# Decayed attention and two gated layers: scores in 64 by 64 quarters of TensorE's array, and two ScalarE steps put ahead of others

## The chip, the cores and the metric

The kernel runs on one core of a Trainium2 chip. The metric is the device time of one execution in microseconds (us); lower is better. The time before is 583.23 us, the median of three runs (583.21 to 583.51). The engines are named as in the profile: PE (TensorE's matmuls), PEld (its weight loads), DVE (VectorE), ACT (ScalarE), POOL (GpSimd) and SP (SyncE, which issues the loads).

## The reference

Blocked linear attention with a decay per head, then two feed-forward layers. Batch 2, 8 heads, 768 tokens, head size 64, so 1536 tokens of width 512 for the layers:

```python
for b in range(nb):                       # blocks of 64 tokens
    intra = einsum('bhic,bhjc->bhij', qb, kb) * Dmask     # the scores
    intra = einsum('bhij,bhjd->bhid', intra, vb)
    inter = einsum('bhid,bhde->bhie', qb * lam_pow, kv_state)
    out[:, :, sl] = intra + inter
    kv_state = lam_block * kv_state + einsum('bhsd,bhse->bhde', kb_dec, vb)
x = act1(x @ w_in) @ w_out                 # act1: 0, x, or (x + 1)^2 / 4 between
x = (sigmoid(x @ w_gate) * (x @ w_val)) @ w_out2
```

## The kernel before

**Attention** works in chunks of 128 tokens (P), not 64. A unit is one pair of heads and three chunks (CU = 3); there are 16 units, and a loop over k = 0 to 7 takes two units in each turn. A turn issues on PE, in this order: `values` (L1041, scores times v, out tile x), `updates` (L998, state sums uu), `values`, then `scores` (L980) of the two units of the next turn, then `queries` (L1061, q times the state, added to x). The scores of turn 0's units are computed ahead of the loop, so that seven turns (k = 0 to 6) hold scores. In turns 6 and 7 matmuls of the first layer (L258 to L260) stand between them, after the scores too; from turn 0 to turn 5 queries follow scores directly. The operands are fp32, and each matmul of the program appears in the trace as two records of a weight load and a matmul: 12 score matmuls are 24 records.

The two heads of a pair lie in the two halves of the partitions (e = 0 and 1), each 64 deep. Scores take as stationary operand 64 partitions and 128 columns, as out tile 128 partitions in a bank per head (s0, s1): the two heads use the upper and the lower half of the array's rows. Queries have 64 partitions and 64 columns of weights, so the two heads use two quarters on a diagonal. Values and updates have 128 partitions and 64 columns: two halves of the array's columns. Groups of these shapes are told apart in the trace by "64*128", "64*64" and "128*64".

SP loads q, k and v of a unit (tile u, `u_load`, L868) into six buffers; its next load into a buffer is issued after the `values` that read it. DVE multiplies scores with the decay (`weigh`, L1009, out pT), scans the states (`states`, L1024, out sc, which queries wait for), and makes a rest of x (`low`, L1077, xl).

**The layers** split every fp32 number into a high and a low part and multiply three times. From group to group of two slices (n0, n1) the second layer runs `pair` generators a and b on PE (L502, through `product`), whose accumulators p0 and p2 are read by ACT or DVE between two products, and `project` (L314). `pair_act` makes what `project` needs: ACT copies the high part gh (L688, L695), ACT makes a sigmoid (L691), DVE makes the rests gl and a product. In one group only (n0 = 20) `forms_third` is worked off beside it, by `along`: each of its ten steps calls `begin` (DVE, L469 and L475: sums of token halves f and rests xt2l), then the step it is given, then `end` (ACT, L472: the high part xt2h of f). Everything is issued by hand in the order of the code; each engine runs its own instructions in that order.

In that group five steps of b go along with five steps of `pair_act`. Three waits of PE stand there: in `pair`, the product of s31 into p0 needs that ACT has copied p0 before (L528), the product of v into p0 after it needs the copy L533, and the product of s24 into p2 needs that DVE has read p2 (L534).

Of the kernel before, what the change touches and what calls it, by code (L numbers as in the profile page):

```python
# [15 lines left out]
B, H, S, D = 2, 8, 768, 64  # L16
NT, DM = B * S, H * D
FF1, FF2 = 2048, 1536
P = 128
# [26 lines left out]
def fused_kernel(ctx: ExitStack, tc: tile.TileContext, qkv, qd, cst, w1, w2, out):  # L46
    nc = tc.nc
    pe, act, dve, pool, sp = nc.tensor, nc.scalar, nc.vector, nc.gpsimd, nc.sync
# [129 lines left out]
    def w_forms_ready():  # L178
        for n in forms:
            if n not in ready:  # L180
                w_forms_split(n)
# [116 lines left out]
    def project(n, t, gs, first, last, now=True):  # L298
        gh, gl = gs
        two = n >= NF1  # L300
        o = 1024 if two else 512
        w_need(n, o)
        w = ws[index[n, o]]
        if first:
            accs.update({j: bank(f"a{n}_{t}_{j}", "a") for j in range(4)})
        for j in range(4):
            js = slice(j * P, (j + 1) * P)
            if two:
                ah, al = (g[j] if isinstance(g, list) else g[:, js] for g in (gh, gl))
                ops = [(ah, w[:, 0]), (ah, w[:, 1]), (al, w[:, 0])]  # L310
            else:
                ops = [(w[:, 0, js], gh), (w[:, 1, js], gh), (w[:, 0, js], gl)]
            for m, (a, b_) in enumerate(ops):
                pe.matmul(accs[j], lhsT=a, rhs=b_, start=(first and m == 0),  # L314
                          stop=(last and m == 2))
        if t == NTT - 1:
            used.update([index[n, o]] if two else [index[n, 0], index[n, o]])
        if last and now:
            flush(n, t)
# [21 lines left out]
    def x_split(t, js):  # L341
        tt = slice(t * TT, (t + 1) * TT)
        for j in js:
            o = part[t][:, j]
            act.activation(xh[:, j, tt], o, AF.Copy)
            dve.tensor_tensor(out=xl[:, j, tt], in0=o, in1=xh[:, j, tt].bitcast(F32),
                              op=ALU.subtract)
# [6 lines left out]
    def go_on():  # L354

        if not (later and later.pop(0)()):
            w_round()
# [45 lines left out]
    def form_split(f, i):  # L403
        hi, lo = x_targets()[i]
        act.activation(hi, f[i], AF.Copy)
        dve.tensor_tensor(out=lo, in0=f[i], in1=hi.bitcast(F32), op=ALU.subtract)
# [31 lines left out]
    def forms_second():  # L438


        x1, x2 = part[0][:, 0:HK], part[0][:, HK:]
        y1, y2 = part[1][:, 0:HK], part[1][:, HK:]
        for o, a, b_ in ((x1, y1, x1), (y1, y2, y1), (y2, y2, x1), (x2, x2, y2)):
            dve.tensor_tensor(out=o, in0=a, in1=b_, op=ALU.subtract)
        return [x1, y2, x2, y1]
# [254 lines left out]
    def single(n, t, between=()):  # L700
        between = iter(between)
        h = hidden(n, t, 0)
        for _ in between:
            pass
        v = hidden(n, t, 512)
        if t == NTT - 1:
            used.update((index[n, 0], index[n, 512]))
        r = rest(f"r{n}_{t}")
        act.activation(r, h, AF.Sigmoid)
        dve.tensor_tensor(out=r, in0=r, in1=v, op=ALU.mult)  # L710
        return r
# [4 lines left out]
    def second_layer(waiting):  # L716

        x_split(1, range(4))
        for p in waiting:
            project(*p)  # L720
        f = []
        later.extend([
            lambda: x_split(2, (0, 1)),
            lambda: x_split(2, (2, 3)) or f.extend(forms_second()),
            lambda: form_split(f, 0) or form_split(f, 2) or True,
            lambda: form_split(f, 1) or form_split(f, 3) or True,
        ])
        fresh = None
        for t in range(NTT):
            for n in range(NF1, NF1 + GF):  # L730
                r = single(n, t)
                if fresh:
                    behind.append(fresh[:2] + (parts(fresh[2], *fresh[:2]),) + fresh[3:])
                if len(behind) == 2:
                    project(*behind.pop(0))
                fresh = n, t, r, n == NF1, n == NF1 + GF - 1
                if (n, t) == (NF1 + GF - 1, NTT - 1):
                    break
                go_on()
                if (n, t) != (NF1, 0):  # L740
                    w_round()
        prog["forms"] = pool
        for n0 in range(NF1 + GF, NF1 + NF2, GF):
            n1 = n0 + 1
            a, b = pair(n0), pair(n1)
            next(a)
            if fresh:
                behind.append(fresh[:2] + (parts(fresh[2], *fresh[:2]),) + fresh[3:])
                waiting, fresh = behind, None
                next(a)  # L750
                next(a)
            thirds = n0 > NF1 + GF
            if not thirds:
                w_round()
            if n0 == NF1 + 2 * GF:
                made = forms_third()

            def along(step):
                begin, end = made.pop(0) if thirds and made else (None, None)
                if begin:  # L760
                    begin()
                x = step()
                if end:
                    end()
                return x

            for _ in range(4 if thirds else 2):
                along(lambda: next(a))
            prog["room"], prog["thirds"] = thirds, thirds
            for p in waiting:  # L770
                w_round()
                project(*p, now=False)
                prog["room"] = False
            flush(p[0], p[1], (0, 1))
            ra, ga = next(a), {}
            flush(p[0], p[1], (2, 3))
            prog["room"] = not thirds
            xa = pair_act(n0, ra, ga)
            for _ in range(5):
                along(lambda: next(b))  # L780
                next(xa)
            w_round()
            project(n0, 0, ga[0], True, False)
            along(lambda: None)
            assert not thirds or not made
            w_round()
            rb, gb = next(b), {}
            xb = pair_act(n1, rb, gb)
            if thirds:
                c = pair_third(n0)  # L790
                for _ in range(5):
                    next(c)
                    next(xb)
                w_round()
                project(n1, 0, gb[0], False, True)
                rc, gc = next(c), {}
                xc = pair_act(n0, rc, gc)
                for _ in range(3):
                    next(xc)
                w_forms_ready()  # L800
                project(n0, 1, ga[1], True, False)
                next(xc)
                w_round()
                next(xc)
                project(n1, 1, gb[1], False, True)
                waiting = []
                for i, n in enumerate((n0, n1)):
                    at = lambda x: [gc[j // 2][x][:, i * HT + j % 2 * P:i * HT + j % 2 * P + P]
                                    for j in range(4)]
                    waiting.append((n, 2, (at(0), at(1)), n == n0, n == n1))  # L810
                continue
            ha = single(n0, 2, xb)
            w_round()
            project(n1, 0, gb[0], False, True)
            ha = parts(ha, n0, 2)
            w_round()
            hb = single(n1, 2)
            w_round()
            project(n0, 1, ga[1], True, False)
            hb = parts(hb, n1, 2)  # L820
            project(n1, 1, gb[1], False, True)
            waiting = [(n0, 2, ha, True, False), (n1, 2, hb, False, True)]
        for p in waiting:
            project(*p)
# [4 lines left out]
    with ExitStack() as actx:  # L829
# [109 lines left out]
        S_ps, U_ps, pT, qs, kd, xs = {}, {}, {}, {}, {}, {}  # L939
# [31 lines left out]
        def scores(i):  # L971
            u = raw_u[i]
            S_ps[i] = []
            for e in range(2):
                s = bank(f"s{i}_{e}")
                S_ps[i].append(s)
            for c in range(CU):
                for e in range(2):
                    r = slice(e * D, (e + 1) * D)
                    pe.matmul(  # L980
                        S_ps[i][e][:, c * P:(c + 1) * P], lhsT=u[1][r, c * P:(c + 1) * P],
                        rhs=u[0][r, c * P:(c + 1) * P],
                        start=True, stop=True,
                    )

        def updates(i):
            u = raw_u[i]
# [92 lines left out]
        with tc.manual_schedule():  # L1080
# [8 lines left out]
            for k in range(nu // 2):  # L1089
                a, b = 2 * k, 2 * k + 1  # L1090
# [160 lines left out]
```

## Time and profile before

| what | before |
|---|---|
| median of three runs | 583.23 us |
| the profiled execution | 583.22 us |
| its span in the profile | 581.4 us |
| PE busy | 576.5 us (99%), 3218 matmul records |
| DVE busy | 454.7 us (78%) |
| ACT busy | 383.4 us (66%) |
| POOL busy | 52.4 us (9%) |
| granted TensorE clock, mean | 0.999 |
| attention | the first 58 us |

The span runs from the first to the last instruction that the profile shows; the execution's time is 1.8 us longer. "Busy" is a share over the whole span, and a matmul's record reaches to its modelled end, so records overlap: what a stage costs is read from the starts of the next stage, or from the chain of work that ended last, which cuts the overlap off.

### The profile page before, as it was taken

Reading aid. Unit: us, or ns where it says so; the run is one execution under the profiler, and the core shown is the slowest. Engines: PE = TensorE matmul, PEld = TensorE weight load, DVE = VectorE, ACT = ScalarE, POOL = GpSimd, SP = SyncE. Lnnn points to the kernel's source line nnn. Section 1 sums busy time; section 2 is a strip of 40 time slices with the busy share of each in tenths; the row PEclk is TensorE's granted clock in tenths of the full one; section 3 lists DMA queues with packets and bytes.
Section 4 is the critical chain, followed back from the end, with each engine's and each line's share of the span. In section 5 each row is a group of like instructions: output and inputs, shape, how many; then the busy total and the mean of one; then the engine's idle time right before and its main releaser. Section 6 shows DMA issues by size and latency. Waiting matters only on the chain.

```text
span 581.4 us, 8399 instructions
## 1 busy us (share of the span) xinstructions
PE 576.5 (99%) x3218; PEld 486.1 (84%) x3218; DVE 454.7 (78%) x772; ACT 383.4 (66%) x675; POOL 52.4 (9%) x60
## 2 busy tenths in 40 slices
PE   9999999999999999999999999999999999999997
PEld 8987888888888888888888888888888898898895
DVE  5988798788897978796898996688876676767555
ACT  4678785996777677777874977756655656655330
POOL 3440000000000000000000002422001112022000
PEclk9999999999999999999999999999999999999999
DMA  8983240022112222221312232222102221220014
GB/s 336 400 324 116 103 144 2 37 104 73 42 72 73 73 73 72 66 79 37 99 48 72 73 108 73 72 74 70 35 5 68 78 73 37 76 70 1 0 61 157
DMA packets 15880, 52.02 MB, mean 89 GB/s; under 512 B 1760, under 2 KB 1888, under 8 KB 15840
## 3 DMA queue, kind: packets, MB, share of 16 engines
q1 hardware_dynamic: 15696, 51.39, 25.1%
q8 instruction: 25, 0.41, 0.3%
q10 hardware_dynamic: 144, 0.10, 0.1%
q14 instruction: 15, 0.12, 0.1%
HBM read 48.33 MB, written 3.15 MB: 89 GB/s over the span
## 4 chain that ended last, share of the span: by engine, by line
PE 99%; DVE 0%; issue 0%
PE a L314 39%; PE p L502 26%; PE t L502 7%; PE h L258 6%; PE h L260 6%; PE h L259 6%; PE s L980 2%; PE x L1041 2%; PE x L1061 2%; PE uu L998 1%; PE z L889 1%; DVE part L336 0%; PE lam L897 0%; DVE zero L928 0%
## 5 line engine op out<-in xcount | busy, mean ns | idle before, releaser
L314 PE MATMUL a<-gh,w 128*128 128x512 f32 x384 | 118.4, 390 | 0.0
L314 PE MATMUL a<-w,gh 128*128 128x512 f32 x288 | 88.8, 390 | 0.0
L314 PEld LDWEIGHTS a<-gh,w 128*128 128x128 f32 x384 | 71.9, 188 | 15.3 <-ACT part L332 0.3
L336 DVE TENSOR_TENSOR part<-part,a 128x512 f32<-128x512 f32 x132 | 82.5, 681 | 2.7 <-PE a L314 2.7
L314 PE MATMUL a<-gl,w 128*128 128x512 f32 x192 | 74.7, 389 | 0.0
L258 PE MATMUL h<-xh,w 128*128 128x512 f32 x160 | 62.7, 392 | 0.0
L314 PEld LDWEIGHTS a<-w,gh 128*128 128x128 f32 x288 | 53.5, 188 | 10.7
L259 PE MATMUL h<-xh,w 128*128 128x512 f32 x160 | 62.3, 389 | 0.0
L260 PE MATMUL h<-xl,w 128*128 128x512 f32 x160 | 62.2, 389 | 0.0
L314 PE MATMUL a<-w,gl 128*128 128x512 f32 x144 | 56.0, 389 | 0.0
L124 ACT ACTIVATE wc<-raw 128x512 uint16<-128x512 uint32 x61 | 47.9, 785 | 10.5 <-DVE wr L135 10.5
L141 ACT ACTIVATE w<-wr 128x512 fp32r<-128x512 f32 x68 | 42.2, 621 | 16.8 <-DVE wr L135 16.6
L163 POOL TENSOR_TENSOR wr<-wr 128x256 f32<-128x256 f32 x16 | 13.3, 833 | 434.7 <-DVE w L145 434.1
L135 DVE CUSTOM_DVE_ANT_0 wr<-wr,wc 128x1024 uint16<-128x1024 uint16 x68 | 47.1, 692 | 5.8 <-ACT wc L125 3.2
L125 ACT ACTIVATE wc<-raw 128x512 f16<-128x512 f32 x61 | 46.9, 769 | 0.0
L145 DVE TENSOR_TENSOR w<-wr,w 128x512 fp32r<-128x512 f32 x65 | 45.2, 696 | 2.0 <-ACT w L141 1.7
L117 ACT ACTIVATE wr<-raw 128x512 f32<-128x512 f32 x68 | 45.0, 662 | 1.5 <-POOL s L172 0.9
L314 PEld LDWEIGHTS a<-gl,w 128*128 128x128 f32 x192 | 36.0, 188 | 7.5
L502 PE MATMUL p<-xh,s 128*128 128x512 f32 x128 | 39.5, 390 | 0.0
L502 PE MATMUL p<-xh,w 128*128 128x512 f32 x128 | 39.4, 389 | 0.0
L502 PE MATMUL p<-xth,s 128*128 128x512 f32 x128 | 39.4, 389 | 0.0
L258 PEld LDWEIGHTS h<-xh,w 128*128 128x128 f32 x160 | 30.0, 188 | 6.6 <-issue 0.2
(157 smaller groups left out, 1140.0 us busy)
## 6 DMA issues: line engine op xcount, KB each, us to landing
raw<-in_w SPq DMA_DIRECT2D x68, 512.0 KB, 3.4
u<-in_qkv SPq DMA_DIRECT2D x24, 384.0 KB, 8.2
out<-part SPq DMA_DIRECT2D x12, 256.0 KB, 2.1
u<-in_qkv SPq DMA_DIRECT2D x3, 768.0 KB, 8.6
part<-in_qkv SPq DMA_DIRECT2D x2, 384.0 KB, 8.4
cs<-in_cst ACTq DMA_DIRECT2D x1, 98.0 KB, 3.7
```

Of the source, the lines that this page charges most:

```text
L117: act.activation(r, hi.bitcast(F32), AF.Copy, scale=2.0 ** -112)
L124: act.activation(limb(U16)[:, :, 0], lo, AF.Copy, scale=2.0 ** -29)
L125: act.activation(limb(F16)[:, :, 1], hi.bitcast(F32), AF.Copy, scale=2.0 ** -60)
L135: eng.tensor_tensor(out=ri, in0=ri, in1=c, op=ALU.add)
L141: act.activation(ws[i][:, 0], tmps[i][0], AF.Copy)
L145: eng.tensor_tensor(out=ws[i][:, 1], in0=r, in1=ws[i][:, 0].bitcast(F32), op=ALU.subtract)
L258: pe.matmul(h, lhsT=wh, rhs=xh[:, k, tt], start=(k == 0), stop=False)
L259: pe.matmul(h, lhsT=wl, rhs=xh[:, k, tt], start=False, stop=False)
L260: pe.matmul(h, lhsT=wh, rhs=xl[:, k, tt], start=False, stop=(k == NP - 1))
L314: pe.matmul(accs[j], lhsT=a, rhs=b_, start=(first and m == 0), stop=(last and m == 2))
L336: dve.tensor_tensor(out=o, in0=o, in1=accs[j], op=ALU.add)
L502: pe.matmul(o, lhsT=a, rhs=b_, start=(start and k == 0 and m == 0), stop=(k == HK - 1 and m == 2), skip_group_check=True)
```

## The change

In `scores` each matmul is cut into two halves of its 64 weight columns (`half_`): the out tile's upper and lower 64 partitions. Per chunk there are four matmuls of 64 partitions by 64 columns, in the order (half 0, head 0), (half 0, head 1), (half 1, head 0), (half 1, head 1), each in a quarter of the array of its own; each still streams 128 columns of q. In the group where `forms_third` runs, `along` now gets b's step and `pair_act`'s step together, so `pair_act`'s instructions are issued before `end` instead of after it.

```diff
             xa = pair_act(n0, ra, ga)
             for _ in range(5):
-                along(lambda: next(b))
-                next(xa)
+                along(lambda: (next(b), next(xa)))
             w_round()
@@ in scores(i)
             for c in range(CU):
-                for e in range(2):
-                    r = slice(e * D, (e + 1) * D)
-                    pe.matmul(
-                        S_ps[i][e][:, c * P:(c + 1) * P], lhsT=u[1][r, c * P:(c + 1) * P],
-                        rhs=u[0][r, c * P:(c + 1) * P],
-                        start=True, stop=True,
-                    )
+                for half_ in range(2):
+                    for e in range(2):
+                        r = slice(e * D, (e + 1) * D)
+                        o = slice(half_ * D, (half_ + 1) * D)
+                        pe.matmul(
+                            S_ps[i][e][o, c * P:(c + 1) * P],
+                            lhsT=u[1][r, c * P + half_ * D:c * P + (half_ + 1) * D],
+                            rhs=u[0][r, c * P:(c + 1) * P],
+                            start=True, stop=True,
+                        )
```

On PE in one turn before, the end of the scores of its second unit, and what follows (s_0 and s_1 are the two heads' banks, "128x128" the out tile and "64x128" one of 64 partitions):

```order
L980 MATMUL s_0_465<-u_132 128x128
L980 MATMUL s_1_466<-u_132 128x128
L1061 MATMUL x_434<-qs_382,sc_97 64x128 x4
L1061 MATMUL x_485<-qs_395,sc_97 64x128 x6
L1041 MATMUL x_485<-pT_400,u_126 64x128 x6
```

The same place in a turn of the changed kernel (its lines stand one or two further):

```order
L981 MATMUL s_0_341<-part_79 64x128
L981 MATMUL s_1_342<-part_79 64x128
L981 MATMUL s_0_341<-part_79 64x128
L981 MATMUL s_1_342<-part_79 64x128
L1063 MATMUL x_306<-qs_241,sc_97 64x128 x4
L1063 MATMUL x_367<-qs_260,sc_97 64x128 x6
```

Each chunk has four score matmuls of half the size where it had two; nothing else moved on PE, where 1972 rows of the order became 2068.

On ACT in the group n0 = 20 before, from b's first step on (q is a copy of an accumulator p, gh the high part for `project`, xt2h and xh the high parts of the token forms f):

```order
L522 ACTIVATE q_0_4031<-p_0_4028 128x512
L688 ACTIVATE gh_0_4041<-q_0_3890 128x512
L472 ACTIVATE xt2h<-f_3906 128x256
L691 ACTIVATE q_1_3891<-q_1_3891 128x512
L528 ACTIVATE q_1_4032<-p_0_4028 128x512
L472 ACTIVATE xt2h<-f_3906 128x256 x2
L695 ACTIVATE gh_1_4042<-q_1_3891 128x512
L533 ACTIVATE q_2_4033<-p_0_4028 128x512
```

The same place in the changed kernel:

```order
L522 ACTIVATE q_0_4127<-p_0_4124 128x512
L688 ACTIVATE gh_0_4137<-q_0_3986 128x512
L691 ACTIVATE q_1_3987<-q_1_3987 128x512
L472 ACTIVATE xt2h<-f_4002 128x256
L528 ACTIVATE q_1_4128<-p_0_4124 128x512
L472 ACTIVATE xt2h<-f_4002 128x256
L695 ACTIVATE gh_1_4138<-q_1_3987 128x512
L472 ACTIVATE xt2h<-f_4002 128x256
L533 ACTIVATE q_2_4129<-p_0_4124 128x512
```

The sigmoid L691 and the copy L695 have each changed places with the token form's high part ahead of them. The orders of DVE, POOL and SP are the same in both kernels.

## Rows read from the trace of the kernel before

**Rows 1.** The page: busy times, and the shares of the last chain.

```profile
PE 576.5 (99%) x3218; PEld 486.1 (84%) x3218; DVE 454.7 (78%) x772; ACT 383.4 (66%) x675; POOL 52.4 (9%) x60
...
PE 99%; DVE 0%; issue 0%
```

**Rows 2.** The last chain over 0 to 60 us, in order: start, us, what.

```profile
8.90 1.58 PE s L980 x24
10.48 1.33 PE x L1061 x20
...
18.42 0.66 PE x L1041 x12
19.08 1.54 PE s L980 x24
20.61 1.33 PE x L1061 x20
21.95 0.81 PE x L1041 x12
22.75 0.58 PE uu L998 x20
...
33.82 1.54 PE s L980 x24
35.35 1.39 PE x L1061 x20
```

**Rows 3.** Line L868 over 27.5 to 28.1 us: one load of u, its landing.

```profile
L868 SPq DMA_DIRECT2D u<-in_qkv x1: 328/328/328, 27.8 to 27.8; - x1
...
DMA to landing us min/median/max: 6.0/6.0/6.0
```

**Rows 4.** Line L980 over 33.5 to 35.4 us: a wait in PE's sequencer.

```profile
L980 PEldq EVENT_SEMAPHORE  x1: 51/51/51, 33.8 to 33.8; - x1
```

**Rows 5.** A stretch: busy us of PE, PEld, DVE, ACT, POOL; clock; DMA share, GB/s.

```profile
29.00:34.00 5.00, 5.00 (x92) 4.59 (x94) 4.65 (x10) 3.02 (x8) 0.69 (x1) 1.00 1.04 410
```

**Rows 6.** DVE in order of time, around 29 to 35 us; idle before in brackets.

```profile
29.80 1.95 DVE L1009 TENSOR_TENSOR pT<-s,DT 128x384 f32<-128x384 f32 x4 [0.28 <-PE s L980]
...
34.39 0.81 DVE L1024 TENSOR_TENSOR_SCAN sc<-ld,uu 128x320 f32<-128x320 f32 x1
```

**Rows 7.** All waits of PE's weight loads from 60 to 420 us: total, times, longest.

```profile
PEld p L502 <- ACT q L533: 0.4, 1, 0.4
PEld a L314 <- ACT part L332: 0.3, 1, 0.3
PEld p L502 <- ACT q L528: 0.2, 1, 0.2
PEld p L502 <- DVE q L534: 0.2, 1, 0.2
```

**Rows 8.** ACT in order of time, 408 to 414 us; idle before in brackets.

```profile
408.58 0.42 ACT L472 ACTIVATE xt2h<-f 128x256 fp32r<-128x256 f32 x1 [1.25 <-DVE f L469]
408.90 0.62 ACT L691 ACTIVATE q<-q 128x512 f32<-128x512 f32 x1
409.43 0.58 ACT L528 ACTIVATE q<-p 128x512 f32<-128x512 f32 x1
...
412.89 0.42 ACT L472 ACTIVATE xt2h<-f 128x256 fp32r<-128x256 f32 x1 [1.44 <-DVE f L469]
413.21 0.62 ACT L695 ACTIVATE gh<-q 128x512 fp32r<-128x512 f32 x1
413.73 0.58 ACT L533 ACTIVATE q<-p 128x512 f32<-128x512 f32 x1
```

**Rows 9.** DVE in order of time, 413 to 416 us.

```profile
413.34 0.42 DVE L475 TENSOR_TENSOR xt2l<-f,xt2h 128x256 fp32r<-128x256 f32 x1 [0.48 <-ACT xt2h L472]
...
415.06 0.68 DVE L534 TENSOR_TENSOR q<-q,p 128x512 f32<-128x512 f32 x1
```

**Rows 10.** PE in the same stretch.

```profile
415.88 0.64 PE L502 MATMUL p<-xh,s 128*128 128x512 f32 x2
```

## The prediction, made before the changed kernel ran

> **What bounds the kernel now.** I read the page's busy times and last chain first: PE is busy 99% of the span and the chain is PE's for 99% of it [rows 1]. So only what PE does, or waits for, can move the end; DVE and ACT count where PE waits for them. Next I asked where PE waits. After attention, from 60 to 420 us, its weight loads wait four times, 1.1 us together [rows 7]; matmuls that are already queued cover a good part of that. The first 58 us are different: the chain there is made of short matmuls, one stage after the other [rows 2], while the DMA engines are full: share 1.04 at 410 GB/s [rows 5]. The change touches this stretch (scores) and three of the four waits (the group at 408 to 416 us).
>
> To read [rows 2]: values (x L1041) are 12 records with two column halves side by side, so six rounds of two. Behind updates, which have the same tile shape, they take 0.66 us: 0.11 us a round. Behind queries, another shape, the same 12 records take 0.81. Going over to a new shape with 64 weight columns thus costs 0.15. Scores: 24 records, two at a time, 12 rounds of 0.11 = 1.32; the row says 1.54, so their entry costs 0.22. Queries: 20 records, 10 rounds = 1.10; the row says 1.33, entry 0.23.
>
> **The change, part by part.** *Rounds.* A quarter matmul streams the same 128 columns as before. Before, two matmuls of half the array made a round, 12 rounds for two units; now 48 records go four at a time, again 12 rounds. If a round stays 0.11 nothing is won or lost here: the array was full before. Values and scores cut the array in two differently and I read the same 0.11 for both; no row shows four at once. Bounds: 0.11 as in these rows, or what PE has been seen to issue: updates pass 20 records in 0.58 us, 29 ns each, so four take 0.116, 12 rounds 1.39 [rows 2]. I take 0.11, since two of the rows nearest in shape agree on it, and keep 0.116 for the range.
>
> [...]
>
> *Entries.* Scores now have the tile shape of queries, and 64 weight columns. Their own entry should cost 0.15 instead of 0.22 (gain 0.07). The entry of the queries behind them, 0.23, should go; what can remain is a slower round of its own, 0.03 in all. Gain per turn: 0.07 + 0.20 = 0.27 (0.20 with rounds of 0.116, 0.30 at best). Queries follow scores directly six times, from 10.48 to 35.35 [rows 2]; the seventh scores stand before first-layer matmuls and gain 0.07 alone. Uncapped: 6 x 0.27 + 0.07 = 1.69 us.
>
> *The cap.* Not all of it passes. In the last such turn the second unit's q and k are loaded by an issue at 27.8 us that lands 6.0 us later, at 33.8 [rows 3], and PE's sequencer holds a wait that ends at 33.8 [rows 4]. The loads fill the DMA engines [rows 5] and land in order of issue, so an earlier PE doesn't make this one land sooner. The scores of that turn end at 35.35 [rows 2]; their second unit is the last 0.66 of it, so it begins at about 34.7 on the chain's scale, some 34.5 by starts. PE can come forward 0.6 to 0.7 there, no more. After the wait: 33.9, six rounds 0.66, a first load of 0.05 that nothing covers: queries begin at 34.6 instead of 35.35, 0.75 earlier. To reach the cap PE needs a lead of 0.6; the turns before give four times 0.27, and with rounds of 0.116 still 0.8, so the rounds' unknown is swallowed here. Of the queries' entry about half (0.1) lies behind their first matmul and comes on top; then 0.07 of the seventh scores: 0.92.
>
> Does DVE follow? Queries need the scan at 34.39, which ends at 35.2 [rows 6], nearly with the queries' start. DVE is dense from 29.80 on (busy 4.65 of 5.00 us, rows 5), and there it waited 0.28 for PE's scores; so it moves with the lead that PE has by then, 3 x 0.27 + 0.07 = 0.88, plus up to 0.27 of the first turn. Its scan then ends near 34.3, before 34.6: no bind. Should it move by its idle 0.28 only, queries start at 35.0 and 0.5 is left of 0.92: a lower end.
>
> The wait for ACT's L332, 0.3 on a weight load [rows 7], hangs on ACT's conversions, which hang on DVE: they come forward by 0.88 to 1.15 where PE comes 0.92. Worth 0 to 0.1; I take 0.04.
>
> *The two swaps on ACT.* Before, copy L533 (413.73) stands behind gh (413.21) behind xt2h (412.89), which waited 1.44 for DVE [rows 8]; gh had nothing to wait for. Now gh fills that idle time, L533 starts at 413.21 and ends at 413.79, 0.52 earlier. Likewise the sigmoid (408.90) goes into the 1.25 idle ahead of 408.58 and L528 starts at 409.0 or so instead of 409.43. So PE's waits of 0.4 for L533 and 0.2 for L528 [rows 7] should both go. What is late next: the product after p0's last one needs DVE's L534. It starts at 415.06 and ends at 415.74 [rows 9], and PE's product began at 415.88 [rows 10], its load having waited for L534 already [rows 7]. L534 stands on DVE behind xt2l at 413.34, which waited for the xt2h of 412.89, which waited for DVE's own sums [rows 8, 9]; the swap moves none of them. So PE can start that product no earlier than about 415.80, at most 0.1 before 415.88; and then with weights that are not loaded ahead, as at the entries above (0.1). Net between -0.05 and +0.14; I take 0, as both rows name the same end. What is swapped costs nothing: xt2h isn't ready before 408.58 and 412.89, and ACT is idle until then.
>
> *Sum.* 0.92 + 0.04 + 0 = 0.96. The profiled execution took 583.22 us (span 581.4 and 1.8 around it); the median is 583.23, so the sum stands against either: 583.22 - 0.96 = 582.26, rounded to **582.3 us**.
>
> **The rivals.** *Smaller gain* (0.10): the 0.23 belongs to the queries' strided weights or their waits, not to the change of shape; then 0.07 a turn is left, 7 x 0.07 = 0.5: 582.7. Against it: values behind updates have no entry, values behind queries have one, with the same operands [rows 2].
>
> *No cap* (0.10): the load at 33.8 comes forward with PE, and all 1.69 passes, 1.7 with L332: 581.5. Against it: a DMA share of 1.04 [rows 5].
>
> *The swap pays* (0.10): L534 ends earlier, for instance since DVE has the sigmoid and gh sooner and shifts; of the 0.8 waited in that group I would see about 0.3 more: 582.0. Against it: DVE's wait of 0.48 for xt2h stays [rows 9].
>
> *Scores twice as fast* (0.03): four tiles do four times the work of one, 12 rounds become six. Behind the cap that is worth 0.33 in the last turn and 0.66 for the seventh scores: 1.9 together, 581.3. Against it: the round is as long for 64 columns as for 64 partitions [rows 2]. [...]
>
> *Slower* (0.07): the four quarters don't run side by side, or PE can't issue them fast enough. The place is the 48 records of each turn. It decides at the point where they take more than 2.87 - 0.15 - 1.12 = 1.60 us, 33 ns a record: above it each turn loses. At two at a time they take 24 rounds, 2.64: about 1.05 lost in each of six turns, 1.25 in the seventh, and 12 rounds more, at least 1.32, in the first scores ahead of the loop: +9, 592 us. For it: no row shows four tiles at once. Against it: two tiles by rows, by columns and on the diagonal all overlap, and updates pass a record in 29 ns [rows 2]. [...]
>
> **How the numbers follow.** The forecast has 0.60, its own range 581.9 to 582.8 (rounds, DVE's lower end, L332). With the rivals: 0.10 + 0.10 + 0.10 + 0.03 + 0.07. The range 581.5 to 583.1 holds the forecast and the three small rivals, 0.90, and leaves out the last two. A measurement of this kernel tells about 0.2% from no change, 1.17 us, so faster means below 582.06: no cap, the swap that pays, the doubled scores and a little of the forecast's lower tail, 0.24. Slower is the last rival and a trifle: 0.08. The rest, 0.68, is within 0.2%: most of the forecast is, by 0.2 us.
>
> **What the profile after would show.** Right: scores of 48 records in about 1.47 on the chain, with queries behind them in 1.10 to 1.13; a new idle stretch or wait of PE in the last turn around 32.9 to 33.9; queries there at 34.6. L533 and L528 gone from PE's waits and L534 still there, with a longer wait. Wrong: scores of 2 us or more on the chain (slower), 0.7 (doubled), queries still at 1.33 (smaller gain), no wait at 33.8 in the last turn (no cap), or PE's product at 415.9 coming 0.3 earlier against its neighbours (the swap pays).

## The result: 0.9% slower, and PE stands still where nothing in the kernel holds it

The changed kernel took 588.48 us (median of 4 runs, 586.98 to 589.62) against 583.37 for the kernel before (4 runs, 583.21 to 583.51): a ratio of 1.0086, 95% interval 1.0057 to 1.0116. The forecast was 582.3 with a range to 583.1. The profiled execution of the changed kernel took 586.98 us, its span 585.1, which is 3.7 more than before. It was the shortest of the four; the two longest have a mean granted clock of 0.996 and 0.994 where the others have 1.000, and no trace shows what more they lost.

The page answers to [rows 1]. PE's busy time hardly moved, so the loss isn't in its work. The chain of after has 5% of DVE, 1% of DMA and 1% of "issue", where before it was PE's alone; of these, DVE's and DMA's shares are no loss of that size, since the chain, followed back, goes over to them at two short waits of PE (0.5 us for L534, shown further below, and 0.7 at 7 us). PE ran 192 matmuls more, each with a weight load, and the instruction queue q8 carried 27 packets (packets, MB, share of the 16 DMA engines' time).

```profile
span 585.1 us, 8783 instructions
PE 575.6 (98%) x3410; PEld 484.7 (83%) x3410; DVE 455.3 (78%) x772; ACT 384.0 (66%) x675; POOL 52.4 (9%) x60
q8 instruction: 27, 0.44, 0.3%
PE 92%; DVE 5%; issue 1%; DMA 1%; ACT 1%; SPq 0%; POOL 0%; DVEq 0%; ACTq 0%; POOLq 0%
```

The queue in the profile of before had

```profile
q8 instruction: 25, 0.41, 0.3%
```

The last chain over the first 62 us shows where the time went (start, us, what). It answers to [rows 2]; scores are now L981, values L1043, queries L1063.

```profile
18.76 0.81 PE s L981 x22
19.57 1.48 issue
21.05 1.03 PE s L981 x26
22.08 1.13 PE x L1063 x20
...
25.25 1.23 PE s L981 x35
26.48 1.17 issue
27.65 0.55 PE s L981 x11
28.30 1.12 PE x L1063 x19
...
31.47 1.47 PE s L981 x48
32.94 0.23 issue
33.17 1.40 PE x L1063 x20
...
38.13 0.94 PE x L1063 x12
39.08 0.84 issue
...
61.46 2.95 PE a L314 x12
```

Four pieces of "issue" make 1.48 + 1.17 + 0.23 + 0.84 = 3.72 us, as much as the span grew. Three lie in the middle of scores or of queries, after the 22nd or the 35th matmul of 48 or the 12th of 20, between two matmuls with the same operands; only the short third one lies where a stage begins. A stop costs more than its idle time: scores that take 1.47 undisturbed took 3.32 with the first (18.76 to 22.08) and 2.95 with the second (25.25 to 28.20). I estimate from such stages that the four cost some 5 us and that the quarters win over 1 us back elsewhere; that the idle time alone equals the growth is chance. In between, the forecast's small figures are there: scores 1.47, queries behind them 1.13.

In those pieces PE neither multiplies nor loads weights, while DVE and ACT go on, the granted clock is 1.00 and the DMA engines are full. The columns are the stretch, its length, busy us of PE, PEld, DVE, ACT and POOL, the clock, the DMA share and GB/s.

```profile
19.60:21.00 1.40, 0.00 (x0) 0.00 (x0) 1.40 (x5) 0.72 (x3) 0.04 (x1) 1.00 1.04 395
26.50:27.60 1.10, 0.00 (x0) 0.00 (x0) 1.10 (x3) 1.10 (x4) 0.56 (x1) 1.00 1.05 404
39.10:39.90 0.80, 0.00 (x0) 0.00 (x0) 0.80 (x3) 0.80 (x3) 0.80 (x2) 1.00 0.95 384
```

What links them is a count. If PE's records in the trace (weight loads and matmuls, with the few entries of its queue) are numbered in order of start, from 0, the first record after each stop is number 705, 961, 1217 and 1473: 256 apart, every time. The queue q8 moved 0.44 MB in 27 packets, 16 KB each, and 27 packets for 6,881 records are one for about 255. So I put the packets of q8 from the trace beside PE's passage over every 256th record:

```
            first record   PE busy   packet of q8   PE goes    stop   from the packet's
            of the block   until     start   end    on at             end to PE going on
after            449       14.09     10.97   12.08   14.09      -          -
                 705       19.57     18.63   19.65   21.05     1.48       1.40
                 961       26.48     25.00   26.03   27.64     1.16       1.61
                1217       32.94     30.54   31.62   33.06     0.12       1.44
                1473       39.08     37.61   38.56   39.92     0.84       1.36
before           449       17.56     13.76   14.84   17.56      -          -
                 705       24.13     20.21   21.33   24.13      -          -
                 961       31.17     26.62   27.72   31.17      -          -
                1217       40.45     33.71   34.73   40.45      -          -
```

Each stop ends 1.4 to 1.6 us after a packet has landed. In the kernel before, PE came to each of these records 2.7 us or more after the packet's end, so some 1.3 us or more to spare. My theory after this view (the supply theory): PE is fed its instructions in blocks of 256 records, the next block is asked for about when the last is begun (no trace shows the asking; in the changed kernel the packet starts 2.9 to 4.6 us after that), and while the loads fill the DMA engines it takes some 6.6 us until it can be used (7.0 from 14.09 to 21.05, 6.6 to 27.64, 5.4 to 33.06, 6.9 to 39.92). Halves used up 256 records in 6.6 to 7.0 us there, quarters in 5.0 to 5.8.

### The profile page after: what moved, and what is told of

Its sections match the earlier page's. It is cut to its first block, busy times and chain, and to the rows that moved or that the text cites. A ratio compares the mean times of both kernels' runs of the same rounds, so it can differ in the third digit from the quotient of the medians.

```text
span 585.1 us, 8783 instructions
## 1 busy us (share of the span) xinstructions
PE 575.6 (98%) x3410; PEld 484.7 (83%) x3410; DVE 455.3 (78%) x772; ACT 384.0 (66%) x675; POOL 52.4 (9%) x60
## 4 chain that ended last, share of the span: by engine, by line
PE 92%; DVE 5%; issue 1%; DMA 1%; ACT 1%; SPq 0%; POOL 0%; DVEq 0%; ACTq 0%; POOLq 0%
PE a L314 36%; PE p L502 23%; PE t L502 7%; PE h L258 6%; PE h L260 6%; PE h L259 6%; PE x L1043 2%; PE s L981 2%; PE x L1063 2%; DVE f L469 1%; DVE part L336 1%; PE uu L1000 1%; DMA u<-in_qkv 1%; DVE xt2l L475 0%; DVE wr L135 0%
```

## Experiments

Two theories stood at the start. Supply, as above; and its rival, that four tiles side by side make PE stall by itself, in the array or its banks. A third suspect, the two swaps on ScalarE, could be taken off at once.

### Which part of the change: scores alone, swap alone

The first kernel undoes the swap:

```
-                along(lambda: (next(b), next(xa)))
+                along(lambda: next(b))
+                next(xa)
```

> The quarters alone, the order on ScalarE as before. Supply theory: in the changed kernel PE stops for 1.2 to 1.5 us in the middle of scores and queries, and each stop begins at PE record 705, 961, 1217 or 1473, so 256 records (16 KB of instructions, the size of one packet of the instruction queue) apart; PE waits there for its own instructions. The swap has no part in that: 588.5 us (587 to 589.6), stops at the same record numbers. Rival, the swap costs it: 583 or a little less.

Measured: 587.51 us (586.72 to 588.07), ratio 1.0071, interval 1.0056 to 1.0086. PE stops at records 705 (1.70), 961 (1.15), 1217 (0.40) and 1473 (0.56). The second kernel has the swap and the old scores.

> The order on ScalarE of the changed kernel, scores in halves as before. Supply theory: the swap is worth nothing or up to 0.1 us: 583.1 to 583.4. Rival, the swap costs it: 587 to 589.

Measured: 583.30 us against 583.25, ratio 1.0001, interval 0.9991 to 1.0011. The whole loss is the quarters', and the swap is worth nothing that can be measured.

### Fewer loads, the same quarters

The loads of units 6 to 15 are left out; these units read unit 4's tiles.

```
+            if i >= NEARLY:
+                raw_u[i] = list(raw_u[4]) if 4 in raw_u else list(raw_u[i - 1])
+                return
             if i not in raw_u:
```

> The kernel before, but q, k and v of units 6 to 15 aren't loaded: these units read unit 4's again (their results are thus other numbers). The DMA engines are then full until about 17 us only, not 37. This is the base for the next kernel. Either theory: PE is the bound without the loads too, 583.0 to 583.4, first-layer products (L314) from about 57.5 us.

> The changed kernel with the same loads left out (units 6 to 15 read unit 4's data). Supply theory: instruction packets no longer wait among loads, no stop of PE at records 961 and 1473 and a small one at most at 705; the quarters then bring what was forecast without the cap by the loads: 1.3 to 1.7 us faster than the kernel with few loads and halves, about 581.7. Rival, four tiles side by side make PE stall by themselves (a conflict inside the array or its banks): the stops stay, 3 to 5 us slower than the kernel with few loads and halves, 587.

Measured: halves 583.30 us (ratio 1.0000, 0.9991 to 1.0010), so the loads don't bound the kernel before. Quarters 584.62 (583.87 to 586.58), ratio 1.0025, interval 1.0014 to 1.0035: neither 581.7 nor 587. The chain of the second says why:

```profile
18.65 0.81 PE s L984 x23
19.46 1.54 issue
21.00 0.97 PE s L984 x25
21.98 1.13 PE x L1066 x20
...
25.15 1.47 PE s L984 x48
26.62 1.12 PE x L1066 x20
```

The stop at record 705 is still there; the others are gone, and the turn from 21.98 to 26.62 takes 4.64 us. The windows of the same kernel (columns as above) put the change of the loads beside it:

```profile
14.00:19.00 5.00, 5.00 (x128) 4.65 (x128) 4.94 (x12) 2.66 (x7) 1.98 (x2) 1.00 1.04 411
25.00:30.00 5.00, 5.00 (x126) 4.63 (x126) 4.90 (x12) 3.58 (x9) 3.12 (x4) 1.00 0.02 5
```

The packet for record 705 started at 18.63, as in the changed kernel, with the engines full since record 449 at 14.03; those for 961 and later started 1.4 us or less after the block before theirs was begun, where it took 2.9 to 4.6 in the changed kernel. The loads ended later than the 17 us that I had expected (read in slices of 1.5 us, the engines were 90% busy or more up to 19.5), too late to help the first stop. So the next kernel leaves out the loads of units 4 to 15 (they read unit 3's), and the same was done to the kernel before.

> The changed kernel, and q, k and v of units 4 to 15 aren't loaded (they read unit 3's; results are other numbers). With units 6 to 15 left out, the stops at records 961, 1217 and 1473 were gone, but the one at 705 stayed at 1.5 us: its packet started at 18.6 us, when the loads had just run out. Now the loads end some 4 us earlier. Supply theory: the packet for record 705 starts by 16 us, no stop anywhere, every turn with quarters takes 4.64 us, 581.7 (581.3 to 582.3), against 583.3 for halves with few loads. Rival, the array or its banks stop at this place: 1.5 us at record 705 again, 584.6.

> The kernel before, and q, k and v of units 4 to 15 aren't loaded (they read unit 3's): the base for the changed kernel with these loads left out, which took 582.41. If PE bounds it as it bounds the kernel before, 583.3 (583.0 to 583.5), and the quarters are worth 0.9 once their instructions are in time. If the loads left out gain by themselves, 582.4, and the quarters are worth nothing.

Measured: quarters 582.41 us (582.17 to 582.67), ratio 0.9984, interval 0.9975 to 0.9993; halves 583.26, ratio 1.0001, interval 0.9991 to 1.0011. No stop at 705 or anywhere: its packet started at 16.0. Same matmuls, same quarters; with the instructions in time they gain 0.85 us. The rival, that the array stops by itself, falls here. The chain shows the short turn, 4.64 from 20.15 to 24.79, and then something else (its 0.40 of "issue" stands ahead of DVE's pT, while PE is busy):

```profile
18.68 1.47 PE s L985 x48
20.15 1.12 PE x L1067 x20
...
24.79 1.12 PE x L1067 x20
...
28.91 0.40 issue
29.30 1.17 DVE pT L1015 x3
...
32.34 0.69 DVE wr L135
...
33.50 0.74 DVE sc L1030
34.37 1.40 PE x L1067 x20
```

From 29.3 on the chain is DVE's, by way of a weight conversion (wr) and up to the scan sc that the queries need. Queries begin at 34.37, 0.98 ahead of the 35.35 of [rows 2], and what PE had gained beyond that is lost in waiting for DVE.

### The same stops in other places of the program

> The changed kernel with 32 narrow matmuls (128x32 weights, 8 columns, 64 records) more in the warm-up, where PE waits for loads anyway. Supply theory: the stops stay at records 705, 961, 1217, 1473, which are now other instructions, 64 records earlier in the program: the first is no longer in the scores (22 matmuls into them) but some 20 records ahead of them, in the values; 587 to 589.5. Rival, the quarters themselves stop PE: the stops stay in the scores, now at records 769 and 1025.

Measured: 587.63 us (2 runs, 587.28 to 587.98). Not all went as expected: the warm-up matmuls came out as two each, as everywhere in this kernel, so the program was shifted by 128 records, not 64, and they took until 8.35 instead of hiding behind the loads, some 3.5 us, which is most of the lost time here. The stages behind them were slower too: from the first scores to the second it took 5.16 us (8.35 to 13.51), against 4.02 in the changed kernel without the loads of units 4 to 15 (4.83 to 8.85); no run tests why. With this late start the packet for 705 was in time. One stop was left, at record 961 again, and it now lies in the updates (L1004), two tiles at a time, whose shape the change doesn't touch:

```profile
25.68 0.81 PE x L1047 x12
26.60 0.45 issue
27.05 0.63 PE uu L1004 x14
```

The packet ended at 25.52, 1.53 ahead of the 27.05. The place in the count decides, not the quarters.

### More records without quarters

The updates of each turn are issued four times over, in the kernel before:

```
-                updates(a)
+                for _ in range(4):
+                    updates(a)
```

> The kernel before, scores in halves, but each turn's updates (20 records of 128x64, 0.58 us) are issued four times over, so that PE gets 60 cheap matmuls more per turn at 29 ns each and no quarter tile: 256 records then take some 5.8 us. The matmuls alone make it 583.3 + 8 x 1.74 = 597. Supply theory: PE stops all the same, at records 705 and 961 while the loads fill the DMA engines, 0.3 to 1.2 us each, in whatever stands there; 598 to 599. Rival, only four tiles side by side stop PE: no stop, 597.

Measured: 597.92 us (2 runs). PE stops at record 705 for 0.05 on the chain and at 961 for 0.54, in the updates and in the queries:

```profile
21.12 0.05 issue
21.18 2.32 PE uu L998 x73
...
26.90 0.54 issue
27.44 0.49 PE x L1061 x3
```

The packets ended at 19.78 and 25.99, 1.40 and 1.44 ahead of PE going on. At 5.5 us for 256 records (21.18 to 26.63) the old tile shapes stop PE too, for less than quarters do at 5.1. The first stop was far below the 0.3 that I had expected as the least.

### Work without records

Two matmuls more ahead of each turn's scores, into banks that the scores overwrite, in the kernel before and in the changed one:

```
+            if i > 1 and not i % 2:
+                for s in S_ps[i]:
+                    pe.matmul(s[:, 0:UT], lhsT=zero, rhs=u[0], start=True, stop=True)
```

> The kernel before with two matmuls more ahead of each turn's scores (128x128 weights of zeros, 384 columns, overwritten by the scores): 0.16 us each and some 0.1 for another tile shape, 0.42 per turn, 7 turns: 583.3 + 2.9 = 586.2 (585.5 to 586.8). It prices the added work for the next kernel.

> The changed kernel with the same two matmuls more per turn. Supply theory: in the four turns where PE stops for its instructions the added work takes the place of the stop, so only three turns pay: 588 + 1.3 = 589.3 (588.3 to 590), and the stops at 705, 961, 1217 and 1473 get shorter by about 0.4 each. Rival, a stop of PE's own that has nothing to do with supply: all seven turns pay, 588 + 2.9 = 590.9, the stops as long as before.

Measured: halves 593.20 us (593.09 to 593.51), ratio 1.0172, interval 1.0157 to 1.0187; quarters 592.32 (591.81 to 592.62), ratio 1.0158, interval 1.0141 to 1.0175. I had mispriced the work: it came out as four matmuls, two for each in the program, and 1.49 us a turn on the chain, not 0.42; no run shows the 0.16 us each that I had put for them, and 1.49 for four is 0.37. That makes the result clearer. Added to halves it costs 9.95 us (583.25 to 593.20); added to quarters only 3.8 (588.48 to 592.32), and the changed kernel with the work is faster than the kernel before with the work. Their chains, halves first:

```profile
22.17 1.49 PE s L979 x4
23.66 1.54 PE s L983 x24
25.20 1.33 PE x L1064 x20
...
68.08 2.95 PE a L314 x12
```

```profile
21.43 1.49 PE s L978 x4
22.92 1.47 PE s L984 x48
24.39 1.11 PE x L1066 x20
...
66.34 2.95 PE a L314 x12
```

Quarters now use up 256 records in 6.3 us (16.73 to 23.03), and in this execution PE doesn't stop at any block. The first products begin at 66.34 against 68.08: 1.74 us gained, with all loads in place. Between the medians it is 0.88: the execution in the profile is the shortest of four for quarters, and the longest of four for halves.

### Quarters only where the packets are in time

If so, quarters outside the stretch of the stops should bring their small gain. One kernel has them for units 12 to 15, one for units 0 to 3 as well, with the old loop for the others:

```
+            if not (i < 4 or i >= 12):
+                for c in range(CU):
+                    for e in range(2):
...
+                return
```

> The changed kernel, but quarters for units 12 to 15 only (the last two turns with scores), halves for the others. Supply theory: packets of halves come in time as before, and the packet for record 1217 lands about 2 us before it is needed: no stop; 0.27 in one turn and 0.07 in the other, 582.9 (582.6 to 583.3). Rival, quarters stop PE wherever they stand: 1.2 to 1.5 us in each of two turns, 585 to 586.

> Quarters for units 0 to 3 and 12 to 15, halves for 4 to 11. Supply theory: the packet for record 449 has about 0.6 us to spare, as in the changed kernel, and from there halves use up 256 records in 7 us, longer than the 6.6 a packet takes: no stop; 582.6 (582.2 to 583.2). If the packet for 705 is late nevertheless: one stop of up to 0.5, 583.0. Rival, quarters stop PE wherever they stand: 586 to 587.

Measured: 583.33 us (583.25 to 583.76), ratio 1.0001, interval 0.9992 to 1.0010; and 583.38 (583.10 to 583.75), ratio 1.0000, interval 0.9991 to 1.0009. Neither has an idle stretch of PE at a block, so quarters in turns of their own cost next to nothing; but the 0.3 to 0.6 us that I had hoped for isn't there. Other waits take it. In the first kernel the scores of units 12 and 13 took 1.47, but the queries behind them wait for DVE's scan, which ends at 35.43, and take 1.40, much as the 1.39 in [rows 2] (DVE in order of time, then the chain):

```profile
34.62 0.81 DVE L1036 TENSOR_TENSOR_SCAN sc<-ld,uu 128x320 f32<-128x320 f32 x1
...
35.58 1.40 PE x L1073 x20
```

In the second kernel the queries of the first turn took 1.12, but the next scores, in halves, took 1.70, so that those behind them begin at 19.00, against 19.08 in [rows 2]: the trace has a load for their second unit landing at 14.56 and PE's wait for it at 14.59, with that unit's first weights behind it at 14.66. The scores of units 12 and 13 took 1.70 instead of 1.47. Record 1217 falls among them, at 34.57, 1.4 us after its packet's end at 33.13; that is the lag of the stops above, so I take it for a stop too short to show as idle time.

```profile
10.45 1.12 PE x L1073 x20
...
13.93 1.70 PE s L980 x24
...
19.00 1.54 PE s L980 x24
...
33.74 1.70 PE s L991 x48
```

None of the kernels run beats the kernel before by more than the measurement can tell, except with loads left out.

## Why the prediction was wrong, step by step

*What bounds the kernel, and the rounds.* The rounds held: 48 records in 1.47, and an undisturbed turn of 4.64 where [rows 2] have 4.91. What failed is the sentence "nothing is won or lost here: the array was full before". It priced the 24 added matmuls of a turn by the array and by the 29 ns a record that updates pass in [rows 2] alone. They also have to be brought in, and at that place PE had about 1.3 us to spare in 7. This term, put at nothing, measured 3.72 us of idle time in the profiled execution, some 5 us with what the stages lost around it. The page had the queue in its third part, 25 packets of 16 KB, and [rows 5] the full DMA engines; I read the latter for what they do to loads only.

*The slower rival.* Its sign came true, by another mechanism. It put the decision at 33 ns a record, and undisturbed scores take 31. The point that decided is per block: 256 records in less time than a packet takes under full loads, some 6.6 us.

*Entries.* Right: 0.27 a turn, as 4.91 less 4.64, where PE isn't stopped and waits for nothing. The sum before the cap, 1.69, is what the profiles of the kernels with added work show: 1.74 to the first products. But the forecast had a load bind in the last such turn alone. In the changed kernel one binds in the second already: the scores from 13.89 took 1.70, with a load for their second unit landing at 14.57.

*The cap.* Its size came out near, but by luck. I named the load that lands at 33.8 as the first thing that would be late. In the kernel with fewer loads there is no such load, and queries in that turn came 0.98 earlier, no more, since they wait for DVE's scan. The step "Does DVE follow?" had the scan's end near 34.3, and it came at 34.24 (33.50 and 0.74 in the chain above); without the load it was the scan that bound. In the shifted kernel, with all loads, PE waits for the scan in that turn too (it ends at 39.29, and queries begin at 39.44), but PE is some 4 us later there than before. How the two caps would share it with all loads, no stop and PE in time can't be seen in any run here.

*The swaps.* Right: 0. L533 and L528 are gone from the waits of PE's weight loads, L332 too, and from 60 us to the end the one wait left for another engine is, against [rows 7],

```profile
PEld p L502 <- DVE q L534: 0.5, 1, 0.5
```

*The sum.* 582.3 was forecast; with fewer loads, so that the instructions are in time, the quarters made it 582.41 (against 583.26). That it lies so near is partly luck, as another cap bound, in a kernel that the forecast wasn't made for. One effect is missing from the forecast: the stops, 3.7 us of idle time in the profiled execution of 586.98, which was the shortest of the four. It is larger than all that was in the sum.

## What to carry to other kernels

A change that makes the same work out of more and shorter instructions has to be priced by the supply too: count PE's records, divide by 256 (6,881 records came in 27 packets here), and ask how long it takes to use up a block where the DMA engines are full. Here PE stopped after blocks used up in 5.0 to 5.8 us (changed kernel, from record 449 on), and not after those that took 6.6 to 7.0 (kernel before) or 6.3 (quarters with added work). A stop of "issue" in the middle of like instructions is the sign; number the records, and if the stops are a fixed count apart, look at the packets of the instruction queue. The short instructions gained 0.85 us where DMA was quiet (583.26 to 582.41) and 0.88 beside added work (593.20 to 592.32); with all loads and nothing beside them they cost 5.1 (583.37 to 588.48).

## What the runs showed of the hardware that I hadn't expected

The instruction queue's packets held 16 KB each (27 of them, 0.44 MB), one for about 255 of PE's 6,881 records; the stops lay 256 records apart, and PE went on 1.3 to 1.6 us after a packet's end in all stops of the five kernels that had them. With the DMA engines full a packet started 2.9 to 4.6 us after the block before was begun (changed kernel, records 705 to 1473), with the loads of units 4 to 15 left out 0.3 to 1.1 after it (records 961 to 1473), and with halves and the same loads left out 0.3 to 0.4 ahead of it (records 705 to 1217). In the changed kernel PE stood still for 0.84 to 1.48 us at three of these four blocks, each time until after the packet had landed.

Adding 1.49 us of work to each of seven turns cost the changed kernel 3.8 us instead of 10: in the profiled execution 256 records then took 6.3 us (16.73 to 23.03), and PE stopped at no block.

Four 64x64 tiles do run side by side: in the changed kernel the four quarters of a round start 6 to 7 ns apart, and a round starts 109 ns after the round before; in the kernel before two halves start 6 to 7 ns apart, and a round starts 112 ns after the round before.
